# A first stage of attention and MLP whose per-engine order is planned inside the kernel, with a changed two-step activation

## The chip, the cores and the metric

The kernel runs on one core of a Trainium2 chip. Its time is the device time of one execution in microseconds; three runs are shown for the kernel before. TensorE (PE), VectorE (DVE), ScalarE (ACT) and GpSimd (POOL) each work through a queue of their own in a fixed order, and transfers are issued from SyncE (SP).

## The reference

Everything is float32. Attention over 2 batches, 8 heads, 768 positions and 64 channels sees, for each position, the keys less than 16 positions away and the 24 block summaries (blocks of 32 positions; the key's summary is a maximum, the value's a mean). Two MLPs follow on the 1536 tokens of width 512, each with 2048 hidden units.

```python
scores_l = scale * (q @ k.T), where |i - j| < 16, else -1e9
scores_s = scale * (q @ k_sum.T) + log(32)          # k_sum: max over a block
a = exp(scores_all - max); a = a / (sum(a) + 1e-9)
x = a @ concat(v, v_sum)                            # v_sum: mean over a block
h = x @ w_in;  g = maximum(h, 0) + alpha * minimum(h, 0);  x = g @ w_out
h = x @ w2_in; g = h * sigmoid(h);                         out = g @ w2_out
```

## The kernel before

Work on the MLPs is done to nearly full float32 precision with three matmuls in place of one: every operand is split into a rounded high part and a low part, and function three issues low x high, high x low, high x high. Each weight part (128 x 512) is loaded raw, put together by three bitwise VectorE steps into w (lines 142, 146, 149), cast to its high part on ScalarE (line 155), and its low part is a subtraction, on GpSimd in the first stage (line 156).

The first stage takes queries in units of 256 positions (block blk, of six) and one pair of heads (p, of four): 24 units. In a unit, scores does 8 small matmuls, which the compiler issues as 16 (line 523): for each 128 queries, head and half of 64 queries, the 24 block summaries and a window of 96 keys side by side, 120 columns. For that the summaries lie ahead of every window in the key tile, and two instructions prepare it (line 465 the maximum, line 471 copies it to the other windows). Then come the scaled and masked scores t (line 531), the maximum nm (540), four exponentials with their sums (548), a small add and a reciprocal (557, 559), the normalization on GpSimd (560), four transposes (566), their copy (568), the values' matmuls (579), and the high and low parts of x (587, 588). Value summaries take two halving adds on GpSimd (482), a sum on VectorE (485), a transpose (491) and four spreading copies on ScalarE (495).

The first chunk (512 of 2048 hidden units) of the first MLP is done in the same stage, block by block: in_k adds the matmuls of one pair's 128 channels, activate does two rectified copies on ScalarE (324, 325), a multiply-add on VectorE (328), a cast (336) and a subtraction (337); out_pair does the second layer. Block 0's first layer runs pair by pair into four PSUM banks while its units are made. Of the eight banks, six serve all of this in rotation and two the scores.

Order is a list of operations sorted by a key in units of one attention unit (the constants AT_..., CONV, BATCH at the top), which the framework's scheduler then places. Weight loads and the second batch's values share two staging buffers; the first three weight parts and the first batch's values go to a region that is free then. After the stage a loop works through the other chunks and the second MLP with tiles of 512 tokens, converting one weight part every few items on VectorE.

Of the kernel before, what the change touches and what calls it, by code (L numbers as in the profile page):

```python
# [10 lines left out]
F32 = mybir.dt.float32  # L11
# [14 lines left out]
AT_KEYS, AT_SUMS, AT_MEANS, AT_SPREAD = -1.1, 1.3, 2.2, 3.2  # L26
AT_EXPS, AT_NORM, AT_TURN, AT_VALUES = 0.1, 0.3, 1.8, 3.2
AT_IN = 5.3
AT_LATER, ITEM_STEP = 3.5, 0.8
CONV, CONV_STEP = -1.4, 0.6  # L30
CONV2, CONV2_STEP = 14.0, 1.5
BATCH, BATCH_STEP = 5.8, 2.0
NQ = 6
STAGE = 2


@with_exitstack
def tile_blocks_attention_mlps(
# [19 lines left out]
    KEYS = P + 2 * PAD  # L58
# [61 lines left out]
    def conv_next(eng):  # L120
# [33 lines left out]
        def rest():  # L154
            nc.scalar.copy(out=hi, in_=w)  # L155
            eng.tensor_tensor(out=lo, in0=w, in1=hi, op=ALU.subtract)
# [5 lines left out]
        return rest  # L162
# [115 lines left out]
    def three(ps, a, b, first, last):  # L278

        (ah, all_), (bh, bl) = a, b  # L280
        nc.tensor.matmul(ps, all_, bh, start=first, stop=False)  # L281
        nc.tensor.matmul(ps, ah, bl, start=False, stop=False)  # L282
        nc.tensor.matmul(ps, ah, bh, start=False, stop=last)  # L283
# [3 lines left out]
    def in_k(u, i, k, ps):  # L287
        l, ch, t0, n, _ = u
        c = slice(i * P, (i + 1) * P)
        hi, lo = pieces[l, ch, 0, k]  # L290
        three(
            ps, (hi[:, c], lo[:, c]), (xh[:, k, t0:t0 + n], xl[:, k, t0:t0 + n]),
            k == 0, k == KT - 1,
        )
# [9 lines left out]
    def activate(u, i, ni, banks):  # L304

# [14 lines left out]
        if l == 0:  # L320
            m = gp.tile([P, 512], F32, tag="m", name="m", bufs=1 if early else 2)
            w = ni * n // len(banks)
# [3 lines left out]
            for j in range(ni):  # L326
                at = slice(j * n, (j + 1) * n)
                nc.vector.scalar_tensor_tensor(  # L328
                    out=g[:, at], in0=m[:, at], scalar=nal[:, f + j:f + j + 1], in1=g[:, at],
                    op0=ALU.mult, op1=ALU.add,  # L330
                )
        else:
            nc.scalar.activation(out=g, in_=banks[0], func=AF.Silu)

        def rest():
            nc.scalar.copy(out=gh, in_=g)  # L336
            (nc.gpsimd if early else nc.vector).tensor_tensor(out=gl, in0=g, in1=gh, op=ALU.subtract)  # L337

        pending.append(rest)
# [80 lines left out]
    def convert(eng):  # L420
        r = conv_next(eng)
        if r is not None:
            pending.append(r)
# [3 lines left out]
    with ExitStack() as scope0:  # L427
# [7 lines left out]
        mask = cst[:, P:]  # L435

        kt_t, vt_t, vs_t, q_t = {}, {}, {}, {}

        def load_k(b, p):

            t = kv.tile([P, NTWO + 1, NB + KEYS], F32, tag="kT", name="kT")
            nc.sync.dma_start(out=t[:, :NTWO, NB:], in_=kT[b, p])
            kt_t[b, p] = t

        def load_v(b, p):
# [5 lines left out]
            vt_t[b, p] = t  # L451
            t = kv.tile([NC, NSUB, P], F32, tag="vs", name="vs")
            vs_t[b, p] = t
            nc.sync.dma_start(out=t[NB:, 0::2], in_=vw[b, p, 0])
            nc.sync.dma_start(out=t[:WIN, 1::2], in_=vw[b, p, 1])
# [7 lines left out]
        def prep_k(b, p):  # L463
            t = kt_t[b, p]
            nc.vector.tensor_reduce(  # L465
                out=t[:, 0, :NB].rearrange("p (n m) -> p n m", n=NTWO),
                in_=t[:, :NTWO, NB + PAD:NB + PAD + P].rearrange("p n (m i) -> p n m i", i=BLOCK),
# [7 lines left out]
        vr_t = {}  # L475

        def prep_v1(b, p):

            t = kv.tile([P, NB], F32, tag="vr", name="vr", bufs=2)
            v = vt_t.pop((b, p)).rearrange("p (n i) -> p n i", i=BLOCK)  # L480
            for w in (BLOCK // 2, BLOCK // 4):
                nc.gpsimd.tensor_tensor(
                    out=v[:, :, :w], in0=v[:, :, :w], in1=v[:, :, w:2 * w], op=ALU.add
                )
            nc.vector.tensor_reduce(out=t, in_=v[:, :, :w], axis=AX.X, op=ALU.add)
            vr_t[b, p] = t

        def prep_v2(b, p):
            s_ = vs_t[b, p]
# [3 lines left out]
            def spread(s0, s1):  # L493
                for at in (s_[:NB, 2 * s0:2 * s1:2], s_[WIN:, 2 * s0 + 1:2 * s1:2]):
                    nc.scalar.activation(
                        out=at,
                        in_=pt[:NB, 0:P].unsqueeze(1).to_broadcast([NB, s1 - s0, P]),
                        func=AF.Copy,
                        scale=1.0 / BLOCK,
                    )  # L500

            spread(0, QB // P)
            return lambda: spread(QB // P, NTWO)

        e_t, pt_t, sums, t_t = {}, {}, {}, {}

        def where(n):
            blk, p = order[n]
            b, j = divmod(blk, BPB)
            return blk, p, b, j  # L510

        def scores(n):
            blk, p, b, j = where(n)
            q_, k_ = q_t.pop((blk, p)), kt_t[b, p].rearrange("p n c -> p (n c)")

            ps = ps_s.tile([P, 2, 512], F32, tag="s", name="sc")
            for i in range(2):
                for h in range(2):
                    hp = slice(h * D, (h + 1) * D)
# [354 lines left out]
```

## Time and profile before

| | us |
|---|---|
| median of 3 runs | 608.24 (608.11 to 608.34) |
| span of the profiled execution | 604.6 |
| the median less the span | 3.6 |
| TensorE busy | 576.8 (95%) |
| VectorE busy | 424.0 (70%) |
| ScalarE busy | 277.5 (46%) |
| GpSimd busy | 72.3 (12%) |

The profile has one execution. Its own time outside the profiler is not recorded, so its span stands for it, and the 3.6 us between span and median are start and end of the program outside the span. A matmul's end is modelled and matmuls overlap, so a busy TensorE says that it had work, not at which rate; for a rate one takes the distance from one start to the next. Times count from the start of the span.

### The profile page before, as it was taken

What the parts mean: (1) busy time and instruction counts of PE and PEld (TensorE: products, weight loads), DVE (VectorE), ACT (ScalarE), POOL (GpSimd) and SP (SyncE); (2) the same over time, 40 slices, a digit from 0 to 9 for tenths busy, and PEclk for the clock granted to TensorE, in tenths of its full rate; (3) what the DMA queues carried; (4) which work ended last, traced back from release to release, by engine and by line L of the source; (5) the groups of instructions that cost most, each with busy time, mean ns of one, the idle gap of its engine ahead of it and who ended that gap; (6) DMA issues with size and microseconds to landing.
All of it is one profiled execution on the core that took longest, in us unless ns stands there. A gap on an engine that the chain in (4) does not pass through costs nothing.

```text
span 604.6 us, 8927 instructions
## 1 busy us (share of the span) xinstructions
PE 576.8 (95%) x3428; PEld 483.5 (80%) x3428; DVE 424.0 (70%) x747; ACT 277.5 (46%) x636; POOL 72.3 (12%) x69
## 2 busy tenths in 40 slices
PE   2777999999999999999999999999999999999997
PEld 1556788999888888888888888888888888888886
DVE  3899979548995484349696879885972499965312
ACT  2768977654543341424544645543621245333200
POOL 2657654232100000000000000000000000000000
PEclk9988999999999999999999999999999999999999
DMA  9958754002351040003022002333130032200112
GB/s 263 341 193 260 231 147 140 2 2 70 140 154 56 0 140 0 1 1 112 28 69 70 1 1 79 131 117 93 32 108 0 1 111 96 73 1 0 54 69 88
DMA packets 31771, 52.54 MB, mean 87 GB/s; under 512 B 2288, under 2 KB 20976, under 8 KB 31728
## 3 DMA queue, kind: packets, MB, share of 16 engines
q1 hardware_dynamic: 31728, 51.97, 27.2%
q8 instruction: 27, 0.44, 0.3%
q14 instruction: 16, 0.13, 0.1%
HBM read 48.82 MB, written 3.15 MB: 86 GB/s over the span
## 4 chain that ended last, share of the span: by engine, by line
PE 82%; DVE 9%; DMA 3%; ACT 2%; SPq 1%; issue 1%; POOL 0%; DVEq 0%; POOLq 0%
PE ps L281 27%; PE ps L282 27%; PE ps L283 27%; DVE w L146 2%; DMA y<-in_w 1%; DVE w L149 1%; DMA vs<-in_vw 1%; DVE w L142 1%; DVE t L531 1%; DVE sm L557 1%; DVE nm L540 1%; PE o L579 1%; DVE kT L465 1%; ACT e L548 1%; DMA raw<-in_w 1%
## 5 line engine op out<-in xcount | busy, mean ns | idle before, releaser
L281 PE MATMUL ps<-xh,wl 128*128 128x512 f32 (+1 forms) x352 | 127.5, 367 | 1.2 <-ACT xh L587 1.2
L282 PE MATMUL ps<-xl,wh 128*128 128x512 f32 (+1 forms) x352 | 127.9, 364 | 0.0
L283 PE MATMUL ps<-xh,wh 128*128 128x512 f32 (+1 forms) x352 | 127.4, 363 | 0.0
L282 PE MATMUL ps<-gl,wh 128*128 128x512 f32 (+1 forms) x240 | 83.3, 348 | 0.0
L283 PE MATMUL ps<-gh,wh 128*128 128x512 f32 (+1 forms) x240 | 82.9, 346 | 0.0
L281 PE MATMUL ps<-gh,wl 128*128 128x512 f32 (+1 forms) x240 | 82.5, 350 | 0.0
L336 ACT CAST gh<-g 128x512 fp32r<-128x512 f32 x96 | 59.3, 622 | 46.2 <-PE ps L283 24.2
L281 PEld LDWEIGHTS ps<-xh,wl 128*128 128x128 f32 x352 | 66.5, 191 | 12.4 <-POOL e L560 1.4
L282 PEld LDWEIGHTS ps<-xl,wh 128*128 128x128 f32 x352 | 67.3, 191 | 10.2 <-issue 0.2
L283 PE MATMUL ps<-wh,gh 128*128 128x512 f32 (+1 forms) x196 | 75.4, 385 | 0.0
L283 PEld LDWEIGHTS ps<-xh,wh 128*128 128x128 f32 x352 | 67.3, 191 | 10.1
L282 PE MATMUL ps<-wl,gh 128*128 128x512 f32 (+1 forms) x196 | 75.4, 385 | 0.0
L281 PE MATMUL ps<-wh,gl 128*128 128x512 f32 (+1 forms) x196 | 75.2, 385 | 0.1
L337 DVE TENSOR_TENSOR gl<-g,gh 128x512 fp32r<-128x512 f32 x84 | 57.5, 687 | 20.7 <-ACT gh L336 20.3
L394 DVE TENSOR_TENSOR y<-ps,y 128x512 f32<-128x512 f32 x48 | 32.8, 689 | 45.4 <-PE ps L283 45.2
L324 ACT ACTIVATE g<-ps 128x512 f32<-128x512 f32 (+1 forms) x50 | 29.0, 579 | 70.8 <-PE ps L283 69.9
L155 ACT CAST wh<-w 128x512 fp32r<-128x512 f32 x64 | 39.3, 622 | 48.0 <-DVE w L149 43.5
L328 DVE SCALAR_TENSOR_TENSOR g<-m,nal,g 128x512 f32<-128x512 f32 (+1 forms) x60 | 41.4, 705 | 25.0 <-ACT m L325 24.9
L281 PEld LDWEIGHTS ps<-gh,wl 128*128 128x128 f32 x240 | 45.2, 189 | 6.6 <-issue 0.5
L282 PEld LDWEIGHTS ps<-gl,wh 128*128 128x128 f32 x240 | 45.4, 189 | 6.1 <-POOL gl L337 0.2
L283 PEld LDWEIGHTS ps<-gh,wh 128*128 128x128 f32 x240 | 45.3, 189 | 5.6
L146 DVE SCALAR_TENSOR_TENSOR w<-raw,w 128x512 uint32<-128x512 uint32 x61 | 44.6, 741 | 0.3
(82 smaller groups left out, 867.1 us busy)
## 6 DMA issues: line engine op xcount, KB each, us to landing
raw<-in_w SPq DMA_DIRECT2D x61, 512.0 KB, 3.8
vs<-in_vw SPq DMA_DIRECT2D x16, 288.0 KB, 5.6
kT<-in_kT SPq DMA_DIRECT2D x8, 480.0 KB, 5.2
q<-in_qT SPq DMA_DIRECT2D x24, 128.0 KB, 4.1
out<-y SPq DMA_DIRECT2D x11, 256.0 KB, 2.0
y<-in_vT SPq DMA_DIRECT2D x4, 384.0 KB, 6.5
y<-in_w SPq DMA_DIRECT2D x3, 512.0 KB, 7.7
raw<-in_vT SPq DMA_DIRECT2D x4, 384.0 KB, 4.5
```

The source lines that it names most:

```text
L142: nc.vector.tensor_scalar(out=w, in0=high, scalar1=3, scalar2=0x3FFFFFFF, op0=ALU.logical_shift_left, op1=ALU.bitwise_and,)
L146: nc.vector.scalar_tensor_tensor(out=w, in0=high, scalar=0xC0000000, in1=w, op0=ALU.bitwise_and, op1=ALU.bitwise_or)
L149: nc.vector.scalar_tensor_tensor(out=w, in0=low, scalar=29, in1=w, op0=ALU.logical_shift_right, op1=ALU.bitwise_or)
L155: nc.scalar.copy(out=hi, in_=w)
L281: nc.tensor.matmul(ps, all_, bh, start=first, stop=False)
L282: nc.tensor.matmul(ps, ah, bl, start=False, stop=False)
L283: nc.tensor.matmul(ps, ah, bh, start=False, stop=last)
L324: nc.scalar.activation(out=g[:, j * w:(j + 1) * w], in_=ps, func=AF.Relu)
L328: nc.vector.scalar_tensor_tensor(out=g[:, at], in0=m[:, at], scalar=nal[:, f + j:f + j + 1], in1=g[:, at], op0=ALU.mult, op1=ALU.add,)
L336: nc.scalar.copy(out=gh, in_=g)
L337: (nc.gpsimd if early else nc.vector).tensor_tensor(out=gl, in0=g, in1=gh, op=ALU.subtract)
L394: nc.vector.tensor_tensor(out=at, in0=src, in1=at, op=ALU.add)
```

## The change

The first stage is no longer a sorted list for the framework's scheduler. Every step (a load, a preparation, one operation of a unit, one conversion step, a pair of hidden rows, an output pair) is declared with its engine, an assumed cost, the steps that it follows, a key, and what it takes and gives back of the buffers (PSUM banks, tiles, staging buffers). The function plan then plays the engines forward: again and again it places the step that can start first, and among those that could start within 0.03 us the one with the lowest key. Conversions on VectorE and work on GpSimd are kept apart by a common lock in the plan, and transfers by an assumed rate. The steps are issued in the order of their planned starts, and that is the order in which each engine runs them.

Beside it:

- The activation is h + (1 - alpha) max(-h, 0): one rectified copy m on ScalarE, and the multiply-add on VectorE reads h from PSUM. This holds for all chunks of the first MLP.
- Summaries stand once in the key tile; scores issues, for each 128 queries and head, one matmul of 24 columns over all 128 queries and two of 96 columns over 64 queries. The keys come unstacked (128 x 800), and a pair's value windows in one load instead of two.
- Value summaries are one sum over 32 positions on VectorE; the halvings are gone. Spreading takes two instructions instead of four.
- The 1e-9 stands in a second column beside each sum; a reduction over two columns replaces the add.
- Blocks 0 and 1 both run their first layer pair by pair, two hidden rows in one PSUM bank, two banks each.
- Two items of the next chunk's first layer run inside the stage instead of one just behind it.

```diff
-AT_KEYS, AT_SUMS, AT_MEANS, AT_SPREAD = -1.1, 1.3, 2.2, 3.2
...
+AT_KEYS, AT_SUMS, AT_MEANS, AT_SPREAD = -1.1, 1.82, 2.2, 1.7
+AT_EXPS, AT_NORM, AT_TURN, AT_VALUES = 0.26, 0.73, 1.37, 3.2
+CONV, CONV_STEP = -1.08, 0.76
+CONV2, CONV2_STEP = 17.32, 2.66
+W_FIRST, W_STEP, W_AHEAD = -98.82, 1.32, -2.52
+SLACK, RATE = 0.03, 0.34
+AHEAD, AT_NEXT = 2, 3.49
...
-                nc.scalar.activation(out=g[:, j * w:(j + 1) * w], in_=ps, func=AF.Relu)
                 nc.scalar.activation(out=m[:, j * w:(j + 1) * w], in_=ps, func=AF.Relu, scale=-1.0)
...
                 nc.vector.scalar_tensor_tensor(
-                    out=g[:, at], in0=m[:, at], scalar=nal[:, f + j:f + j + 1], in1=g[:, at],
-                    op0=ALU.mult, op1=ALU.add,
+                    out=g[:, at], in0=m[:, at], scalar=nal[:, f + j:f + j + 1],
+                    in1=ps[:, j * n % w:j * n % w + n], op0=ALU.mult, op1=ALU.add,
                 )
...
-            nc.vector.tensor_copy(
-                out=t[:, 1:, :NB], in_=t[:, 0:1, :NB].to_broadcast([P, NTWO, NB])
-            )
...
+                for h in range(2):
+                    hp = slice(h * D, (h + 1) * D)
+                    nc.tensor.matmul(
+                        ps[:, h, i * NC:i * NC + NB],
+                        q_[hp, i * P:(i + 1) * P],
+                        k_[hp, KEYS:KEYS + NB],
...
-                            ps[s * SUB:(s + 1) * SUB, h, i * NC:(i + 1) * NC],
+                            ps[s * SUB:(s + 1) * SUB, h, i * NC + NB:(i + 1) * NC],
                             q_[hp, i * P + s * SUB:i * P + (s + 1) * SUB],
-                            k_[hp, w0:w0 + NC],
+                            k_[hp, w0:w0 + WIN],
...
+        room = {"sc": 1, "mm": 6, "t": 3, "e": 3, "pT": 2, "q": NQ, "k": 4, "v": 4, "vr": 2,
+                "raw": STAGE, "w": 2, "g": 1, "gh": 3}
...
+        for n in range(3 * CF + STAGE):
+            t = W_FIRST + n * W_STEP if n < 2 * CF else max(W_FIRST + n * W_STEP, CONV2 + (n - 2 * CF) * CONV2_STEP - W_AHEAD)
+            load(("W", n), t, load_next, size=0.52, after=[("W", n - 1)] * (n > 0),
+                 take=["raw"] * (n >= y_w.shape[1]))
...
+            step(("sc", *g), "PE", 0.8, [("K", b, p), ("q", *g)], k + AT_SC, scores, *g,
+                 take=["sc"], give=["q"] + ["k"] * last)
+            step(("mk", *g), "DVE", 0.58, [("sc", *g), "cst"], k + AT_MASK, masked, *g,
+                 take=["t"], give=["sc"])
...
+            step(("e", *g), "POOL", 0.95, [("rs", *g)], k + AT_NORM, normalize, *g, lock=True)
+            step(("pt", *g), "PE", 0.45, [("e", *g)], k + AT_TURN, turn, *g,
+                 take=["mm"], give=["e"])
...
+            step(("cv", n), "DVE", 1.65, [("W", n)] + [("cv", n - 1)] * (n > 0), t, bits, n,
+                 take=["w"], give=["raw"] * (n >= y_w.shape[1]), lock=True)
...
+        def plan():
+            end, free, hold = {}, dict.fromkeys(("SP", "PE", "ACT", "DVE", "POOL"), 0.7), {}
...
+                        at = max([free[e], *(end[x] for x in after)])
+                        for r in take:
+                            at = max(at, sorted(hold[r])[take.count(r) - 1])
+                        if lock:
+                            at = max(at, locked)
...
+                        t0 = min(at for at, _ in found)
+                        at, s = min(((at, s) for at, s in found if at <= t0 + SLACK), key=lambda x: x[1][:2])
...
+        with tc.manual_schedule():
+            for _, _, f, a in plan():
+                f(*a)
```

## Rows read from the trace of the kernel before

**Rows 1.** Busy time by stretch: span, its length, then per engine (instructions), clock, DMA share, GB/s.
```profile
0.00:40.00 40.00, 22.81 (x220) 17.40 (x221) 28.80 (x56) 20.82 (x70) 19.25 (x23) 0.96 0.93 278
40.00:64.00 24.00, 17.13 (x250) 13.47 (x250) 23.96 (x48) 21.18 (x81) 15.05 (x14) 0.93 0.72 220
64.00:104.00 40.00, 39.50 (x450) 34.76 (x451) 35.06 (x70) 31.68 (x96) 22.27 (x20) 1.00 0.61 176
```

**Rows 2.** The chain of waits: start, length (us), what.
```profile
15.52 7.75 DMA y<-in_w
23.29 1.19 DVE w L142
...
75.95 3.81 DMA raw<-in_w
...
102.46 0.63 PE sc L523 x14
```

**Rows 3.** Timeline of TensorE where it is full: start, length, what.
```profile
117.63 0.64 PE L523 MATMUL sc<-kT,q 64*64 64x120 f32 x16
118.20 0.69 PE L579 MATMUL o<-pT,vs 120*64 120x64 f32 x16
118.82 0.65 PE L566 MATMUL pt<-cst,e 128*120 128x128 f32 x4
119.40 0.69 PE L579 MATMUL o<-pT,vs 120*64 120x64 f32 x16
120.01 0.38 PE L281 MATMUL ps<-xh,wl 128*128 128x256 f32 x1
120.24 0.28 PE L282 MATMUL ps<-xl,wh 128*128 128x256 f32 x1
120.35 0.28 PE L283 MATMUL ps<-xh,wh 128*128 128x256 f32 x1
```

**Rows 4.** TensorE's groups, 0 to 64 us: busy, mean ns; idle before, releasers.
```profile
L523 PE MATMUL sc<-kT,q 64*64 64x120 f32 x224 | 13.1, 346 | 13.5 <-DVE kT L465 5.7 <-DVE t L531 3.4 <-DVE vr L485 3.3
L566 PE MATMUL pt<-cst,e 128*120 128x128 f32 x44 | 9.3, 350 | 7.2 <-POOL e L560 5.2 <-POOL wl L156 1.3 <-DVE xl L588 0.7
L579 PE MATMUL o<-pT,vs 120*64 120x64 f32 x144 | 8.6, 280 | 2.2 <-DVE xl L588 1.9 <-ACT m L325 0.3
...
L281 PE MATMUL ps<-xh,wl 128*128 128x256 f32 x18 | 5.2, 377 | 1.2 <-ACT xh L587 1.2
```

**Rows 5.** Transfers, GB/s in each microsecond from 0 to 40 us.
```profile
GB/s 0 0 147 352 342 315 327 281 267 298 321 405 306 253 325 377 337 343 386 289 297 309 407 414 343 373 348 257 295 336 343 368 373 176 116 12 0 86 291 303
```

**Rows 6.** Groups of other engines by shape, 0 to 130 us.
```profile
L531 DVE SCALAR_TENSOR_TENSOR t<-sc,cst 128x480 f32<-128x480 f32 x24 | 15.5, 646 | 6.6 <-PE sc L523 6.5
...
L328 DVE SCALAR_TENSOR_TENSOR g<-m,nal,g 128x256 f32<-128x256 f32 x18 | 11.8, 693 | 1.8 <-ACT m L325 1.8
...
L557 DVE TENSOR_SCALAR sm<-sm 128x4 f32<-128x4 f32 x24 | 9.0, 374 | 4.7 <-ACT e L548 4.7
...
L588 DVE TENSOR_TENSOR xl<-o,xh 128x256 fp32r<-128x256 f32 x21 | 8.6, 412 | 0.4 <-ACT xh L587 0.3
...
L465 DVE TENSOR_REDUCE kT<-kT 128x24 f32<-128x768 f32 x8 | 7.5, 943 | 6.4 <-DMA kT<-in_kT 6.4
...
L324 ACT ACTIVATE g<-ps 128x512 f32<-128x512 f32 x7 | 4.1, 590 | 3.4 <-PE ps L283 2.9 <-POOL gl L337 0.5
...
L471 DVE COPY kT<-kT 128x144 f32<-128x144 f32 x8 | 2.9, 358 | 0.0
...
L485 DVE TENSOR_REDUCE vr<-y 128x24 f32<-128x192 f32 x4 | 1.4, 344 | 2.4 <-POOL y L482 2.4
```

**Rows 7.** VectorE's conversion steps by shape: 0 to 64 us, then 150 to 200 us (two rows).
```profile
L146 DVE SCALAR_TENSOR_TENSOR w<-raw,w 128x512 uint32<-128x512 uint32 x6 | 6.6, 1100 | 0.0
...
L146 DVE SCALAR_TENSOR_TENSOR w<-raw,w 128x512 uint32<-128x512 uint32 x10 | 6.8, 684 | 0.0
L142 DVE TENSOR_SCALAR w<-raw 128x512 uint32<-128x512 uint32 x8 | 4.1, 515 | 2.0 <-DMA raw<-in_w 1.9
```

More of the change, by code (lines that the diff above doesn't have):

```diff
@@ L290, in in_k @@
         hi, lo = pieces[l, ch, 0, k]
-        three(
+        return three(
             ps, (hi[:, c], lo[:, c]), (xh[:, k, t0:t0 + n], xl[:, k, t0:t0 + n]),
-            k == 0, k == KT - 1,
+            k == 0 if first is None else first, k == KT - 1, first is not None,
         )
@@ L304, in activate, with activation @@
     def activate(u, i, ni, banks):
+        one, two, *rest = activation(u, i, ni, banks)
+        one()
+        two()
+        pending.extend(rest)
+    def activation(u, i, ni, banks):
         l, ch, t0, n, _ = u
@@ L730, in seq_item, with step, load @@
-        def seq_item():
-            need(CF if seq[0][1] is in_item else 2 * CF)
-            item()
-        def more_loads():
-            for _ in range(CF):
-                ask(None)
+        where = {g: k for k, g in enumerate(order)}
+        steps = []
+        def step(name, engine, cost, after, key, f, *a, take=(), give=(), lock=False, size=0):
+            steps.append((key, len(steps), name, engine, cost, after, f, a, take, give, lock, size))
+        def load(name, key, f, *a, size, after=(), take=()):
+            step(name, "SP", 0.6, after, key, f, *a, take=take, size=size)
@@ new lines, in tile_blocks_attention_mlps, with first_in, whole_in @@
+        acc, acts = {}, {}
+        def first_in(blk, p, i):
+            if blk not in acc:
+                acc[blk] = [ps_mm.tile([P, 512], F32, tag="mm", name="ps") for _ in range(CF // 2)]
+            for i in range(0, CF, 2) if i is None else [i]:
+                ps = acc[blk][i // 2]
+                in_k(units[blk], i, p, ps[:, :QB], p == 0)
+                in_k(units[blk], i + 1, p, ps[:, QB:], False)
+        def whole_in(blk, i):
+            ps = ps_mm.tile([P, 512], F32, tag="mm", name="ps")
+            acc.setdefault(blk, {})[i // 2] = ps
+            for j in range(2):
+                for k in range(KT):
+                    in_k(units[blk], i + j, k, ps[:, j * QB:(j + 1) * QB])
@@ new lines, in tile_blocks_attention_mlps, with next_in @@
+        ahead = []
+        def next_in(f):
+            ps = ps_mm.tile([P, 512], F32, tag="mm", name="ps")
+            for k in range(KT):
+                in_k(units[NBLK], f, k, ps)
+            ahead.append(ps)
+        for f in range(AHEAD):
+            step(("nx", f), "PE", 2.72, [("lo", 3 * CF - 1)] + [("x", blk, p) for blk in range(TB // QB)
+                 for p in range(NPAIR)] + [("nx", f - 1)] * (f > 0), NG + AT_NEXT + f, next_in, f, take=["mm"])
+        def plan():
+            end, free, hold = {}, dict.fromkeys(("SP", "PE", "ACT", "DVE", "POOL"), 0.7), {}
+            for r, n in room.items():
+                hold[r] = [0.0] * n
+            left = {e: sorted(s for s in steps if s[3] == e) for e in free}
+            locked, wire, out = 0.0, 0.0, []
+            while any(left.values()):
+                best = None
+                for e, todo in left.items():
+                    found = []
+                    for s in todo[:60]:
+                        key, _, name, _, cost, after, f, a, take, give, lock, size = s
+                        if any(x not in end for x in after):
+                            continue
+                        if any(len(hold[r]) < take.count(r) for r in take):
+                            continue
+                        at = max([free[e], *(end[x] for x in after)])
[3 more added lines that the diff above has]
+                            at = max(at, locked)
+                        if size:
+                            at = max(at, wire - 6.5)
+                        found.append((at, s))
+                    if found:
+                        t0 = min(at for at, _ in found)
+                        at, s = min(((at, s) for at, s in found if at <= t0 + SLACK), key=lambda x: x[1][:2])
+                        if best is None or at < best[0]:
+                            best = at, s
+                at, s = best
+                key, _, name, e, cost, after, f, a, take, give, lock, size = s
+                left[e].remove(s)
+                out.append((at, s[1], f, a))
+                free[e] = at + cost
+                if lock:
+                    locked = at + cost
+                for r in take:
+                    hold[r].remove(min(hold[r]))
+                end[name] = at + cost + (0.25 if e == "PE" else 0.12)
+                if size:
+                    wire = max(wire, at + 1.4) + size / RATE
+                    end[name] = wire + 0.9
+                for r in give:
+                    hold[r].append(end[name])
+            return sorted(out, key=lambda x: x[:2])
@@ L780, in tile_blocks_attention_mlps @@
     ps_o.append(ctx.enter_context(tc.tile_pool(name="ps_o", bufs=2, space=bass.MemoryType.PSUM)))
+    for f in range(AHEAD):
+        activate(units[NBLK], f, 1, [ahead[f]])
+        convert(nc.vector)
+        rests()
     due = 0.0
```

397 lines of the change are left out of this document (196 added, 201 removed).

## The prediction

> **What bounds the kernel now.** Start with the busy time by stretch [rows 1]. From 64 us on TensorE is busy in 39.5 of 40 us, and it stays so to the end of the program; before 40 us it is busy in 22.8 of 40 us, and VectorE, at 23.96 of 24 us between 40 and 64, is full. The chain of waits [rows 2] says the same in order of time: a weight's transfer ends at 23.3 us, VectorE's conversion starts there, VectorE's steps make up most of the chain until 84 us, and from 102.5 us it is TensorE alone. So the program is TensorE-bound with a late start, and the question is how late.
>
> A busy TensorE early on is not one at its rate, so I count work instead. At full rate [rows 3] a score group takes 0.57 us (117.63 to 118.20), a values group 0.61, a transpose group 0.58 and elsewhere about 0.4 (I take 0.5), a 256-column matmul 0.12 (120.35 from 120.24). Up to 64 us TensorE issued [rows 4] 224/16 = 14 score groups, 11 transpose groups, 9 values groups and 52 matmuls of 256 columns (18 of line 281's, 17 each of lines 282 and 283): 8.0 + 5.5 + 5.5 + 6.2 = 25.2 us, with four small transposes about 26. **The lag at 64 us is 64 - 26 = 38 us.** After that TensorE waits 0.5 us in the next 40, so nearly every microsecond taken from the lag comes off the end. The whole first stage is 24 x (0.57 + 0.5 + 0.61) + 576 x 0.12 + 1.6 = 111 us of TensorE.
>
> Of the 38 us only some must be. At 30 us the sum of the transfer rates [rows 5] is 9.05 MB. The first two blocks need four pairs of k, v, v-windows and two q tiles (1.64 MB each) plus the constants and four first-layer weight parts (2.4 MB): 9.0 MB. They were all there near 30 us, yet 34 us later, at 64 us, only 52 of the 96 matmuls that they feed had run.
>
> **The change part by part.** VectorE first, since it holds the chain.
> - Copies of the key maxima to the other windows (line 471) go: 8 x 0.358 = 2.9 us [rows 6].
> - The two halvings on GpSimd go and VectorE's sum reads 768 columns instead of 192. The nearest row is the maximum over 768, 0.943; the sum over 192 takes 0.344 [rows 6]: 8 x 0.6 = 4.8 us more. GpSimd loses 16 instructions, which no longer sit between a transfer and the sum.
> - The small add before the reciprocal takes 374 ns [rows 6]. It becomes a reduction of eight numbers, bounded by today's 0.374 and by nearly nothing; taken 0.17, half of a sum over 192 columns, which is mostly fixed cost: 24 x 0.2 = 4.9 us less.
> - The activation's multiply-add, 24 in this stage, reads h from PSUM. Today 693 ns with both inputs in SBUF; the nearest with one input in PSUM and 256 columns is the low half of x, 412 [rows 6]. Bounds 0.41 and 0.69, taken 0.43: 6.3 us less.
> - The planner holds conversions and GpSimd's work apart. The second conversion step took 1100 ns before 64 us and 684 when GpSimd is quiet [rows 7]; over three steps about 0.6 us, 12 times: 0 to 7 us less, taken 5.
> VectorE's stage thus loses 14 us (it is busy 88 up to 104 us [rows 1]), but before 64 us only some 5 of 53 (eight copies, eleven small adds, nine conversions, less six longer sums). Work removed is not the main effect; order is.
>
> ScalarE loses one Relu per pair (0.59 [rows 6], 7 us in 12 pairs) and half of its spreading instructions; in later chunks 36 more Relus go. I cost these at nothing: ScalarE is busy 31.7 of 40 us while TensorE is full [rows 1]. Without that cover it is the 7 us. In return the PSUM bank stays held through VectorE's step, about 0.4 us longer, hidden by the other banks; uncovered 12 x 0.4 = 5 us. The accumulators of block 0 (four banks) become two banks for each of blocks 0 and 1: four of six either way.
>
> On the queue of transfers each pair's v-window loads become one and keys shrink from 480 to 400 KB: 0.3 MB in the first eight units, about 1 us; the first weight is now asked for ahead of pair 1's values, and the loads for the second batch follow the buffers as they come free. Nothing else is put ahead of a load that the first unit needs.
>
> The scores are the cost on TensorE. A unit has 16 issued matmuls of 120 columns; it will have 16 of 96 and 8 of 24 over all 128 output columns. Bounds: 0.57 (work alone: 16 x 120 against 16 x 96 + 8 x 24 x 2 columns) and 0.57 x 24/16 = 0.86 by count. Taken 0.75, nearer the count since 24 columns is short of every row seen: +0.18 x 24 = **+4.3 us** (0 to 7).
>
> Now the order. (a) First phase, to the end of blocks 0 and 1's first-layer matmuls. Data are there at 30 us. VectorE's part [rows 6, 7] is 8 x 2.0 for units (mask 0.65, the maximum over the same columns as much, two small steps of 0.17, low half 0.41), 4 x 1.9 for key maxima and sums, and 5 x 1.9 for conversions (0.515 + 2 x 0.684): 33 us. It can start when the first key tile has landed, at 4.7 us, so 38 us at best. That leaves it no idle time. In the first 40 us it now idles 11.2 [rows 1], 4.7 of them for the first key; of the other 6.5 I allow 4, so 42. TensorE has then done 8 x 1.86 + 0.8 + 96 x 0.12 = 27 us: lag 15. (b) Until the second-layer weights are converted, which I put at about 48 (three more parts through two buffers, a chain wait of 3.81 at most for one [rows 2], half overlapped), only units 8 to 11 and block 2 can run, 13 us of work in bits as VectorE feeds it: 5 us more. (c) From there on, per unit, TensorE has 1.86 + 2.9 (24 matmuls of 0.12) = 4.7 us, and VectorE 2.0 plus a share of keys and sums 0.5, conversions 0.8, multiply-adds 0.4 and output copies 0.35 = 4.1: TensorE full, with little to spare. **Lag 20 against 38: 18 us less.** Bounds: 11 (38 us, nothing in b) and 33 (52 us, 8 in b).
>
> Sum: -18 + 4.3 = -13.7. The profiled execution has a span of 604.6 us; the median of the runs is 608.24, so 3.6 us lie outside the span and stay. Span 591, time **594.5 us**. The likeliest case alone: 587 to 601.
>
> What follows the stage is left as it is: two items of the next chunk run ahead instead of one, and TensorE is full there already.
>
> A rule against the change, beside the rows. After a group of small tiles the first full matmul starts the next one 0.23 us later instead of 0.12 (120.01 to 120.24 [rows 3]): about 0.11 us to change over. The new score group goes from 64x128 tiles to 64x64 tiles twice, three change-overs inside a unit that had none. The Trainium skill, TensorEngine Tiling (Array Packing), Key Properties, says that a change of tiling mode, not just of tile, drains TensorE. By that rule the sum would be 0.33 x 24 = 8 us for the drains on top, 602.5; by the count alone 594.5.
>
> **The rivals.**
> 1. The drains (above): 3 x 0.11 x 24 = 8 us on top of the 4.3: 602.5. For: the 0.11 us is seen. Against: values and transposes, of different tiles too, follow each other from 118.20 to 120.01 at 0.6 each [rows 3], as quick as where they stand alone. Chance 0.10.
> 2. VectorE stays the bound of the first 64 us. For: it loses only 5 of 53 us there, and its sums grow. Then the lag falls by those 5 and by some 4 from order, less 4.3: about 604. Against: block 0 and 1's matmuls need only eight units, and nothing forces the other work ahead of them. Chance 0.15.
> 3. Slower, by one mechanism: VectorE stands behind a conversion whose weight has not landed. From the fourth weight on, nine conversions and four v loads share two buffers. The chain shows one such wait of 3.81 us at 75.95 [rows 2], and behind it on VectorE's queue stand the masked scores and maxima of the next units, for which TensorE, ScalarE and GpSimd wait. The order is fixed by planned landing times, so a plan that is early blocks again and again. At 3.81 each the gain is gone with the fourth; with six, 23 us against 13.7: 617. Against: the transfers are busy 0.61 of the time from 64 to 104 us [rows 1], so there is room on the wire, and only one such wait is on the chain of a kernel with the same two buffers. Chance 0.13.
> 4. No change: the order gets TensorE full earlier by just what the scores cost (lag 34): 608. Chance 0.05.
>
> **How the numbers follow.** Forecast 0.57; with rivals 1 and 2 faster in 0.82; within 0.2% (1.2 us, about what a measurement of this kernel can tell from no change) 0.05; slower 0.13. The range of 8 in 10 runs from 584 (lag 12 with scores at 2 us) to 607, which takes in rivals 1 and 2 and leaves out rival 3 and the ends.
>
> **What would show it.** Right: 256-column matmuls of the first layer start near 15 us, when one unit's chain and one weight can be through; counted as above, the lag at 64 us is near 20; the small reduction stands near 0.17, the multiply-add near 0.43; a score group takes 0.75. Wrong: VectorE idle ahead of the first conversion step with a transfer as the releaser several times (rival 3); VectorE full to 64 us with under 90 matmuls of 256 columns done (2); a score group near 1.0 (1). What would make the prediction wrong altogether is a wait on PSUM banks, of which two serve transposes, values and means while the accumulators hold four, as they do now.

## The result, and the profile after

The changed kernel takes 613.57 us (median of 4 runs, 612.1 to 614.3) against 608.17 for the kernel before beside it: a ratio of 1.0085, 95% interval 1.0061 to 1.011. It is slower where 594.5 was forecast, and the time lies outside the range of 584 to 607. The profiled execution has a span of 611.9 us against 604.6, 7.3 more, where the medians differ by 5.4. In every execution that has both numbers on record (all but the profiled one of the kernel before) the time is 1.7 to 1.9 us longer than the span. So the profiled execution before took some 606.4 us, less than its median: half of the 3.6 us that the prediction adds to the span is that, and not start and end of the program.

Busy time by stretch after, columns as in [rows 1]:

```profile
0.00:40.00 40.00, 26.46 (x278) 20.66 (x279) 20.81 (x45) 19.06 (x64) 7.80 (x12) 1.00 0.88 247
40.00:64.00 24.00, 24.00 (x303) 20.52 (x299) 19.00 (x42) 16.33 (x59) 7.38 (x7) 0.86 0.50 163
64.00:104.00 40.00, 38.54 (x462) 33.85 (x463) 34.55 (x74) 32.34 (x104) 22.07 (x19) 0.91 0.65 190
```

Against [rows 1] the two engines have changed places: from 40 to 64 us VectorE is busy 19.0 us where it was full, and TensorE is full where it was busy 17.1. Read as shares this is just what was wanted. The next two views say what TensorE is full with. The chain of waits after (start, length, what) runs early through TensorE's scores, where [rows 2] has VectorE's steps:

```profile
21.33 0.56 PE sc L533 x4
21.89 0.53 PE sc L544 x8
22.41 0.55 PE sc L533 x4
22.97 0.53 PE sc L544 x8
```

And the timeline of TensorE where it runs at the full granted clock, as in [rows 3]:

```profile
99.58 0.41 PE L533 MATMUL sc<-kT,q 64*128 64x24 f32 x4
99.91 0.40 PE L544 MATMUL sc<-kT,q 64*64 64x96 f32 x8
100.24 0.41 PE L533 MATMUL sc<-kT,q 64*128 64x24 f32 x4
100.57 0.40 PE L544 MATMUL sc<-kT,q 64*64 64x96 f32 x8
100.90 0.39 PE L287 MATMUL ps<-gh,wl 128*128 128x256 f32 x1
101.12 0.28 PE L288 MATMUL ps<-gl,wh 128*128 128x256 f32 x1
```

From the first start to that of the full matmul behind it, a unit's scores take 100.90 - 99.58 = **1.32 us, where they took 0.57** and 0.75 was forecast. TensorE's groups from 0 to 64 us, as in [rows 4]:

```profile
L533 PE MATMUL sc<-kT,q 64*128 64x24 f32 x102 | 13.3, 337 | 9.5 <-DVE kT L488 5.7 <-issue 1.9 <-DMA q<-in_qT 1.8
L544 PE MATMUL sc<-kT,q 64*64 64x96 f32 x200 | 12.5, 332 | 0.0
L287 PE MATMUL ps<-xh,wl 128*128 128x256 f32 x28 | 9.8, 350 | 0.0
...
L596 PE MATMUL pt<-cst,e 128*120 128x128 f32 x40 | 8.0, 335 | 0.0
L612 PE MATMUL o<-pT,vs 120*64 120x64 f32 x144 | 7.5, 260 | 1.1 <-ACT pT L601 1.1
```

Counted as in the prediction, with 1.32 for a score group and 0.2 for each of four small transposes: 12.6 units x 1.32 + 10 x 0.5 + 9 x 0.61 + 84 x 0.12 + 0.8 = 38.0 us of work, a lag of 26 at 64 us (38 before, 20 forecast). The order did bring TensorE forward, if by less than forecast; 84 full matmuls stand there instead of 52. The same count up to 104 us gives a lag of 62.1 to 104 = 41.9 before and 104 - 72.9 = 31.1 after. So the order is worth 10.8 us where the stage gets full, the scores cost 24 x (1.32 - 0.57) = 18.0, and 18.0 - 10.8 = **7.2 us**, against the 7.3 by which the span has grown. The prices are rounded, so the last tenth is luck, but the same count up to 104 us also comes near the spans of the first three runs below: 1.9, 5.1 and 4.6 us less than before, measured 2.1, 5.2 and 4.7.

VectorE's groups by shape up to 130 us, which answer to [rows 6, 7]:

```profile
L150 DVE SCALAR_TENSOR_TENSOR w<-raw,w 128x512 uint32<-128x512 uint32 x11 | 9.6, 870 | 0.3
...
L347 DVE SCALAR_TENSOR_TENSOR g<-m,nal,ps 128x256 f32<-128x256 f32 x16 | 6.9, 475 | 3.4 <-ACT m L341 3.4
...
L146 DVE TENSOR_SCALAR w<-raw 128x512 uint32<-128x512 uint32 x11 | 5.5, 504 | 2.5 <-DMA raw<-in_w 2.5
...
L507 DVE TENSOR_REDUCE vr<-y 128x24 f32<-128x768 f32 x4 | 3.8, 946 | 1.2 <-DMA y<-in_vT 1.2
...
L583 DVE TENSOR_REDUCE rs<-eps 128x4 f32<-128x8 f32 x23 | 3.5, 152 | 2.5 <-ACT e L574 2.3
```

The small reduction takes 152 ns (0.17 forecast), the multiply-add 475 (0.43), the sum over 768 columns 946 (0.943), the second conversion step 870, only in part down to its quiet 684: it is 692 in all five conversions before 64 us and 909 in the nine from there to 130.

SyncE's transfers after, in order of issue:

```profile
17.19 0.33 SPq L120 DMA_DIRECT2D y<-in_w  x1
...
31.84 0.42 SPq L120 DMA_DIRECT2D y<-in_w  x1
35.04 1.87 SPq L472 DMA_DIRECT2D raw<-in_vT  x2
48.48 0.33 SPq L464 DMA_DIRECT2D kT<-in_kT  x1
49.39 0.37 SPq L120 DMA_DIRECT2D raw<-in_w  x1
```

The third weight is asked for at 31.84 us and the fourth, the last that the first layer needs, at 49.39: between them two loads of the second batch's values take both staging buffers. The kernel before had asked for its second weight at 15.52 us, for its third at 17.74 and for the fourth here:

```profile
22.71 3.43 SPq L116 DMA_DIRECT2D raw<-in_w  x1
```

### The profile page after: what moved, and what is told of

Same layout as the page of the kernel before. It is cut to its first block, busy times and chain, and to the rows that moved or that the text cites. A ratio compares the mean times of both kernels' runs of the same rounds, so it can differ in the third digit from the quotient of the medians.

```text
span 611.9 us, 9208 instructions
## 1 busy us (share of the span) xinstructions
PE 593.4 (97%) x3620; PEld 499.5 (82%) x3620; DVE 415.3 (68%) x743; ACT 252.6 (41%) x568; POOL 56.1 (9%) x53
## 4 chain that ended last, share of the span: by engine, by line
PE 93%; issue 3%; DMA 1%; DVE 1%; SPq 0%; POOL 0%; POOLq 0%; ACT 0%
PE ps L287 28%; PE ps L288 27%; PE ps L289 27%; PE sc L533 3%; PE sc L544 3%; PE pt L596 2%; PE o L612 2%; DMA q<-in_qT 1%; POOL gl L356 0%; DVE w L150 0%; POOLq L976 0%; DVE t L556 0%; ACT pT L601 0%; DVE y L426 0%; DVE g L347 0%
## 5 line engine op out<-in xcount | busy, mean ns | idle before, releaser
L287 PE MATMUL ps<-xh,wl 128*128 128x512 f32 (+1 forms) x352 | 130.5, 371 | 0.0
L289 PE MATMUL ps<-xh,wh 128*128 128x512 f32 (+1 forms) x352 | 128.7, 366 | 0.0
L287 PEld LDWEIGHTS ps<-xh,wl 128*128 128x128 f32 x352 | 68.4, 194 | 10.8 <-issue 0.2
L288 PEld LDWEIGHTS ps<-xl,wh 128*128 128x128 f32 x352 | 68.6, 195 | 9.8
L341 ACT ACTIVATE m<-ps 128x512 f32<-128x512 f32 x48 | 28.7, 597 | 86.3 <-PE ps L289 86.0
L347 DVE SCALAR_TENSOR_TENSOR g<-m,nal,ps 128x512 f32<-128x512 f32 (+1 forms) x60 | 37.2, 637 | 27.1 <-ACT m L341 27.1
L574 ACT ACTIVATE e<-t,nm 128x120 f32<-128x120 f32 x96 | 36.7, 384 | 18.3 <-DVE nm L567 16.2
```

What stands on the lines that cost most here:

```text
L287: i = nc.tensor.matmul(ps, all_, bh, start=first, stop=False, skip_group_check=again)
L288: nc.tensor.matmul(ps, ah, bl, start=False, stop=False, skip_group_check=again)
L289: nc.tensor.matmul(ps, ah, bh, start=False, stop=last, skip_group_check=again)
L347: nc.vector.scalar_tensor_tensor(out=g[:, at], in0=m[:, at], scalar=nal[:, f + j:f + j + 1], in1=ps[:, j * n % w:j * n % w + n], op0=ALU.m ...
L574: nc.scalar.activation(out=e[:, u, :], in_=t[:, u, :], func=AF.Exp, bias=nm[:, u:u + 1], accum_out=sm[:, u, 0:1],)
```

## The experiments: the scores

The theory: a unit's scores now go back and forth between two tile shapes, and TensorE pays at each change. The rival: it pays by the number of instructions, 24 instead of 16. The first three runs keep the changed kernel and alter the scores alone.

**All 24-column matmuls first**, then all of 96 columns: one change in a unit instead of three, the same 24 instructions, the same plan.

```diff
             for i in range(2):
                 for h in range(2):
                     hp = slice(h * D, (h + 1) * D)
                     nc.tensor.matmul(
                         ps[:, h, i * NC:i * NC + NB],
...
+            for i in range(2):
                 for h in range(2):
```

> The changed kernel with one edit: in a unit's scores all four 24-column matmuls come first, then the eight of 96 columns; the same 24 issued instructions, but one change between tile shapes inside the group instead of three. Drain theory (each change of shape costs about 0.2 us, which is what 1.32 us less the 0.57 of the old group leaves for it): the group falls to about 0.95 us, 24 x 0.37 = 9 us less, time near 604.5. Count theory (0.055 us for each of 24 instructions): group 1.32, time 613.5 within 1. Order theory (the loss is waiting and not the scores): the group may fall but the time stays within 2 of 613.5.

606.92 us, ratio 0.9974 (0.9952 to 0.9996). TensorE's timeline of this kernel:

```profile
113.57 0.63 PE L533 MATMUL sc<-kT,q 64*128 64x24 f32 x8
114.12 0.56 PE L545 MATMUL sc<-kT,q 64*64 64x96 f32 x16
114.61 0.69 PE L613 MATMUL o<-pT,vs 120*64 120x64 f32 x16
```

A unit takes 114.61 - 113.57 = 1.04 us, 0.28 less for two changes less: 0.14 each. Over 24 units that is 6.7 us, and the ratio fell by 0.0111, 6.7 us.

**Small tiles for the short matmuls**: 64 of the 128 queries at a time, so that all have the 64x64 shape. That makes 32 instructions and no change inside a unit; the plan stays.

```diff
-                        ps[:, h, i * NC:i * NC + NB],
-                        q_[hp, i * P:(i + 1) * P],
...
+                    for s in range(2):
...
+                            ps[s * SUB:(s + 1) * SUB, h, i * NC:i * NC + NB],
+                            q_[hp, i * P + s * SUB:i * P + (s + 1) * SUB],
```

> The changed kernel with the 24-column matmuls cut to 64x64 tiles as the windows' are: 32 issued instructions a unit instead of 24, no change of shape inside the group. Drain theory: group about 0.6 to 0.75 us, 24 x 0.6 = 14 us less, time near 599. Count theory: 32 x 0.055 = 1.76 us, 24 x 0.44 = 10.5 us more, time near 624. Order theory: within 2 of 613.5.

**600.68 us, ratio 0.9853 (0.9827 to 0.9879).** Its timeline of TensorE:

```profile
100.58 0.31 PE L534 MATMUL sc<-kT,q 64*64 64x24 f32 x8
100.72 0.38 PE L545 MATMUL sc<-kT,q 64*64 64x96 f32 x8
100.91 0.26 PE L534 MATMUL sc<-kT,q 64*64 64x24 f32 x8
101.00 0.37 PE L545 MATMUL sc<-kT,q 64*64 64x96 f32 x8
101.30 0.39 PE L287 MATMUL ps<-gh,wl 128*128 128x256 f32 x1
```

101.30 - 100.58 = 0.72 us: with a third more instructions than the changed kernel a unit takes 0.60 us less, 14.4 us over 24; the ratio fell by 0.0232, 14.1 us. The count theory falls. Of the 0.75 us that a unit had grown, 0.28 went with two changes of shape, 0.32 with the third and with the 64x128 tile itself (these two runs don't part them), and 0.15 stays. (The median itself fell by 12.9 us and the span by 12.5; the ratios are taken to the kernel before beside each run.)

**Summaries stacked ahead of each window again**, in the changed kernel's plan: 16 instructions of 120 columns.

```diff
+            nc.vector.tensor_copy(
+                out=t[:, 1:, :NB], in_=t[:, 0:1, :NB].to_broadcast([P, NSUB - 1, NB]))
...
-                            k_[hp, w0:w0 + WIN],
+                            k_[hp, 2 * (2 * j + i) + s],
```

> The changed kernel with the scores of the kernel before: the summaries are copied ahead of each of 12 stacked windows of 96 keys, and a unit has 16 issued matmuls of 120 columns in 64x64 tiles. Eight VectorE copies of some 0.35 us come back and a pair's keys are 590 KB instead of 400. Drain and count theories alike: group 0.57 us, 24 x 0.75 = 18 us less, 2 to 4 us back for copies and loads, time near 597. Order theory: within 3 of 613.5.

602.0 us, ratio 0.9881 (0.9854 to 0.9907). A unit takes 0.57 us again (101.25 to 101.82), 18 us less in all; only 12.4 are measured. The count puts the rest into a larger lag, 37.3 at 104 us where the changed kernel has 31.1. That this comes from the copies on VectorE, and not from the larger loads of keys, is not shown.

**The new scores and layout alone in the kernel before.**

> The kernel before with the new scores alone (24 and 96 columns, keys and value windows laid out for them, no copies of summaries), order and activation as before. If the scores cost 0.75 us a unit more: about 10 units lie where TensorE is full, 7.5 us more, less what VectorE saves with the copies, time 613 to 616; if they cost nothing that shows (order theory): within 2 of 608.2.

631.12 us, ratio 1.0358 (1.0332 to 1.0384): 22 us slower, well above the 613 to 616 expected. The price of 1.32 a unit gives 18 of them (in its timeline too the four rows of a unit start 0.33 us apart: 100.91, 101.25, 101.57, 101.91), and the count up to 140 us has a lag of 49.4 against 43.5 before. Where one of its units is broken up, groups of other sizes stand between changes of shape:

```profile
124.44 0.40 PE L515 MATMUL sc<-kT,q 64*128 64x24 f32 x2
124.77 0.39 PE L526 MATMUL sc<-kT,q 64*64 64x96 f32 x6
```

The next matmul, of the full shape, starts at 125.09. So two matmuls of 24 columns take 0.33 us and six of 96 take 0.32, and in the changed kernel four of 24 and eight of 96 take 0.33 each. With small tiles eight of 96 take 0.19 with the same shape behind them (100.72 to 100.91) and 0.30 with another (101.00 to 101.30). In these rows a short group that ends in a change of shape takes 0.30 to 0.33 us, whichever of these it holds, and four such groups make the 1.32. Only the eight of 24 columns in the first run take more, 0.55 (113.57 to 114.12).

## The experiments: the order

With small tiles a unit costs 0.72 us, what the prediction had taken (0.75), so that kernel should have come near 594. It took 600.7 and, **measured again** beside the last run below, 599.5.

> The run with small tiles for the short matmuls once more, as the measure for the run with halved v loads on the same chip: a ratio near 0.985 and 599 to 602 us by the theory that the changes between tile shapes cost the scores their time; a ratio near 1 if the first measurement was a chance of its chip.

Ratio 0.9849 (0.9818 to 0.988): it holds. The windows of the first of these two runs, with two stretches of 4 us:

```profile
0.00:40.00 40.00, 25.33 (x482) 20.82 (x482) 27.61 (x61) 24.87 (x87) 11.01 (x15) 1.00 0.94 268
40.00:64.00 24.00, 19.57 (x382) 16.67 (x379) 22.75 (x52) 21.00 (x72) 12.20 (x12) 0.96 0.88 264
64.00:104.00 40.00, 37.34 (x457) 34.65 (x456) 32.87 (x65) 26.41 (x80) 19.51 (x17) 0.89 0.44 129
...
68.00:72.00 4.00, 1.65 (x52) 1.35 (x50) 3.90 (x9) 2.09 (x4) 1.39 (x2) 1.00 0.39 113
72.00:76.00 4.00, 3.69 (x61) 2.84 (x53) 3.90 (x7) 4.00 (x17) 2.06 (x2) 0.56 0.71 214
```

TensorE's work counted as above is again 38.0 us at 64 us (16 units x 0.72 + 13 x 0.5 + 12 x 0.61 + 96 x 0.12 + 1.2), lag 26. At 104 us it is 70.8, lag 33.2: 8.7 less than before, 3.6 of dearer scores, so 5.1 us; the span fell by 5.2 (599.4). VectorE is nearly full until 64 us and transfers are too. At 64 us this stands on VectorE's timeline:

```profile
63.95 0.65 DVE L557 SCALAR_TENSOR_TENSOR t<-sc,cst 128x480 f32<-128x480 f32 x1
68.00 0.43 DVE L146 TENSOR_SCALAR w<-raw 128x512 uint32<-128x512 uint32 x1 [3.40 <-DMA raw<-in_w]
```

VectorE waits 3.4 us for a weight that the chain has in flight for 8.43 us from 59.55. TensorE runs dry from 68 to 72 (1.65 busy of 4) and then works at a granted clock of 0.56, near the lower of its two levels (1.2 of 2.4 GHz). The profiled execution of the second run, with a span of 598.7, has this otherwise: VectorE waits 1.81 us for the same weight and 2.53 for an earlier one, TensorE is busy 3.36 of 4 us from 68 to 72, and the clock from 72 on is 1.00. So neither the dry stretch nor the slow one behind it is needed for the time of this kernel. Theories for what holds the stage: late weights, the two staging buffers, VectorE's amount, the rate of the loads. Each was tried, from the small-tile kernel unless said.

**Weights earlier**: a load follows the issue of the one before, not its landing, and the second batch's values take one staging buffer at a time. First with small tiles, then with the changed scores, then with small tiles and the scores' planned cost at 0.6 instead of 0.8.

```diff
-            load(("W", n), t, load_next, size=0.52, after=[("W", n - 1)] * (n > 0),
+            load(("W", n), t, load_next, size=0.52, after=[("Wi", n - 1)] * (n > 0),
...
-                load(("vt", b, p), t + 1.5, load_vt, b, p, size=0.39, take=["raw"])
+                load(("vt", b, p), t + 1.5, load_vt, b, p, size=0.39, take=["raw", "rv"])
```

> The second experiment's kernel (summaries in 64x64 tiles) with two edits of the planner's rules: a weight part's load has to follow only the issue of the one before it, not its landing, and the second batch's v loads may hold one of the two staging buffers, not both. Load theory (both buffers go to v loads at about 33 us, so the fourth weight part is asked for at 38.7 us and the eighth at 59.6, and the second layer waits for them; the chain there is transfers and conversions from 34 to 68 us): the fourth follows the third at once, the eighth is converted near 50 us, 7 to 10 us less, time 591 to 594. Rival (VectorE is full from 32 to 64 us anyway, 0.9 of the time, and sets the pace): within 2 of 600.7.

> The changed kernel, its scores as they are, with the same two edits of the load order alone. Load theory in full: 5 to 8 us less, time 606 to 609. If the scores alone set the pace (TensorE is on the chain from 12 us to the end): within 2 of 613.5. So this tells how much of the changed kernel's own loss is the loads'.

> The fifth kernel with the planner's price of a score group at 0.6 us, as measured with small tiles, instead of 0.8, so that the plan's order is made for the group that runs. Theory that a wrong price misorders the queues: 1 to 3 us under the fifth. Rival (0.2 us in a group changes nothing that matters): within 1 of the fifth.

605.36 (0.9953, 0.9925 to 0.9982), 616.12 (1.0121, 1.0081 to 1.0161) and 606.29 (0.996, 0.9937 to 0.9984): with small tiles slower than without the edit, with the changed scores not faster (the intervals overlap).

**Staging buffers freed**: the second batch's values in two tiles of their own; then with the issue order too; then both with the changed kernel's scores.

```diff
-                t = stage.tile([P, 512, 2], F32, name="raw")...
+                t = kv.tile([P, S], F32, tag="vx", name="vx", bufs=2)
```

> The small-tiles kernel with the second batch's values loaded to two tiles of their own instead of the two staging buffers that the weights use. Buffer theory (13 loads go through two buffers between 30 and 85 us, the eighth weight part is asked for at 59.6 us and TensorE is short of work from 60 to 80 us): weights flow, TensorE is busier from 60 to 80 us, 3 to 8 us less, 593 to 598. Rival (the loads are not what is short there): within 1.5 of 600.7.

> The kernel of the run before with a weight's load following the issue and not the landing of the one before it. Buffer theory: as good as the run before or 1 to 3 us better, 591 to 597. Rival (VectorE, given more conversions early, makes the units late, as in the fifth run): 603 to 607.

> The changed kernel, scores as they are, with both edits of the loads (own place, issue order). Buffer theory: 2 to 5 us less than 613.5, 608 to 612. Rival (the scores keep TensorE on the chain whatever the loads do): within 2 of 613.5.

606.39 (0.9934, 0.9911 to 0.9957), 611.46 (1.0032, 1.0004 to 1.006) and 626.69 (1.0278, 1.0231 to 1.0325): slower again. In the last, the window from 40 to 104 us has a granted clock of 0.76 with TensorE busy 59.90 of 64 us.

**Less work on VectorE**: sums over 8 of 32 positions, which leaves out three quarters of every value mean; then the halvings back on GpSimd.

```diff
-  step(("vr", b, p), "DVE", 0.87, [("vt", b, p)], k + AT_SUMS, sum_v, b, p, BLOCK,
+  step(("vr", b, p), "DVE", 0.87, [("vt", b, p)], k + AT_SUMS, sum_v, b, p, BLOCK // 4,
```

> The second experiment's kernel (small tiles) with the value sums taken over the first 8 of each 32 positions alone: it leaves out three quarters of the value means, in the same order of steps, and nothing is put in their place. VectorE has 8 x 0.6 = 4.8 us less to do, six of the eight sums before 70 us. VectorE theory (it is busy 30.1 of 32 us from 32 to 64 us and sets the pace there): 3 to 5 us less, time 596 to 598. Rival (loads or the order set it): within 1 of 600.7.

> The small-tiles kernel with the two halvings of the values back on GpSimd, as before the change, as planned steps of 1.7 us under the common lock, and VectorE's sum over 192 columns. VectorE theory: 8 x 0.6 us of VectorE go, but a halving stands between a landing and the sum, and GpSimd blocks conversions: 1 to 4 us less, 597 to 600. Rival: no gain or up to 3 us more, the sum being the longer way.

600.11 (0.9829, 0.9788 to 0.9869) and 601.79 (0.9858, 0.9826 to 0.9889). The short sum takes 0.34 us instead of 0.95, 4.8 us less over eight with the plan unchanged, and the time doesn't answer beyond the intervals.

**The v loads in halves**, plan unchanged.

```diff
-            nc.sync.dma_start(out=t[NB:], in_=vw[b, p])
+            for s in (slice(0, NSUB // 2), slice(NSUB // 2, NSUB)):
+                nc.sync.dma_start(out=t[NB:, s], in_=vw[b, p, :, s])
```

> The kernel of the run with small tiles for the short matmuls (600.7 us), with each v load of two heads' windows cut into two loads of half its bytes, and the plan unchanged. If the stage's loads are what holds it until about 70 us, because the long packets of the merged load land slowly (9.1 us for 576 KB, where the kernel before moved its smaller loads at 278 GB/s in the first 40 us), the halves land earlier and the run takes 596 to 599 us. The rival, by which the order of the steps and not the rate of the loads holds the stage: within 1 us of the same kernel with whole loads, run beside it.

599.08 us, ratio 0.9841 (0.9814 to 0.9868), within 1 us of its measure: the rival. The loads land a little earlier but the rate in the first 40 us is 263 GB/s against 268. From its profile's list of DMA issues (KB each, us to landing; 576 KB in 8.6 with whole loads), and two of its windows:

```profile
vs<-in_vw SPq DMA_DIRECT2D x16, 288.0 KB, 7.2
```

```profile
64.00:72.00 8.00, 6.44 (x73) 5.67 (x73) 5.13 (x14) 5.12 (x16) 2.74 (x3) 0.79 0.76 202
72.00:80.00 8.00, 6.95 (x123) 6.07 (x113) 7.83 (x17) 8.00 (x29) 4.69 (x6) 1.00 0.64 203
```

The half-rate stretch from 72 us on is not there (the clock is 0.79 from 64 to 72), but nor is it in the second run of the kernel with whole loads, so the halves can't be credited with that. The time is the same.

**The old activation.** First with its own costs and bank release in the plan, then with the halvings on GpSimd too; then the same old instructions in exactly the small-tile kernel's order; last the new activation alone in the kernel before.

```diff
+                nc.scalar.activation(out=g[:, j * w:(j + 1) * w], in_=ps, func=AF.Relu)
...
-                    in1=ps[:, j * n % w:j * n % w + n], op0=ALU.mult, op1=ALU.add,
+                    in1=g[:, at], op0=ALU.mult, op1=ALU.add,
```

> The small-tiles kernel with the activation of the kernel before (two Relus on ScalarE, the multiply-add on SBUF alone; the PSUM bank given back after ScalarE). If reading h from PSUM holds banks behind VectorE's full queue (the eighth experiment was 0.4% slower with it): 1 to 3 us less, 598 to 600. If it only saves: ScalarE gets 7 us more and VectorE up to 24 x 0.2 us: 601 to 604.

> Both edits of the two runs before on the small-tiles kernel. VectorE theory and the bank theory together: 595 to 599; if each costs: 602 to 606.

> The small-tiles kernel with the old activation's instructions and the plan left as it is (same prices, same order of steps on every engine). If the 12 us of the eleventh run are the activation itself: about 612. If they are the other order that the plan made of its prices: 600 to 604.

> The kernel before with the new activation alone: one Relu less for each pair, the multiply-add reads h from PSUM. Costed at nothing on ScalarE and 0.27 us less on VectorE for each of 24 multiply-adds, which are on the chain only in places: time 606 to 608.5. If the PSUM banks held longer cost what I put as uncovered: up to 5 us more, 613.

613.19 (1.0046, 1.0014 to 1.0079), 620.15 (1.0156, 1.012 to 1.0192), 603.0 (0.9902, 0.9866 to 0.9937) and 611.79 (1.0042, 1.0024 to 1.006). In one order the new activation is worth 0.0049 of 608, some 3 us, with intervals that just overlap. The first and the third run hold the same instructions and differ in their order alone: 0.0144, 8.8 us. In the kernel before, where the framework's scheduler places the steps, the new activation gains nothing and costs 2.6 us; whether by the order or by the banks held longer is not parted.

## Why the prediction was wrong

- **The step that failed** is the term of the scores, "Taken 0.75 ... +4.3 us (0 to 7)". It measured 0.75 us on top of 0.57, so +18.0, outside both bounds. The bounds were made from columns and from count, and the measure refutes count: 32 instructions take 0.72 us and 24 take 1.32. What the prediction had beside them as a rule, and gave 0.10, was the mechanism of at least 0.28 of the 0.75 us: tiles of another shape don't follow each other freely. The Trainium skill, TensorEngine Tiling (Array Packing), Key Properties, says that a change of tiling mode drains TensorE; the trace agrees, with 0.14 us for each of the two changes that could be taken out by themselves. Rival 1 was mis-sized as well: 8 us on top, against 13.7.
- The evidence against it was misread. Values and transposes do follow each other at 0.6, but a group of 16 that pays one change can't show what a group of 4 or 8 pays for each (sixteen of 96 columns ahead of another shape take 0.49 us in the first run, eight take 0.33 in the changed kernel).
- **The order**, "Lag 20 against 38: 18 us less", had the mechanism right and the size wrong: 12 us by 64 us, and 10.8 left at 104. The phase (a) that was to end at 42 us had its 96th matmul of 256 columns only near 56 us with small tiles and near 67 us after; at 42 us 24 of them had run, as many as before. The first such matmul stood at 28.4 us, not near 15. "Data are there at 30 us" was read from the kernel before (with the new keys of 400 KB in the sum; its own 480 make it some 1 us later) and did not hold for the new plan, which asked for the third weight at 31.84 us and for the fourth at 49.39, since two loads of values had taken both staging buffers at 35.04. The sentence "Nothing else is put ahead" looked only at what the first unit needs. With small tiles the sum of VectorE's steps left out that units beyond the eight run in between, 16 in the first 64 us.
- **TensorE early.** Phase (a) took VectorE as its limit and TensorE's work at full-rate prices. After, the chain of waits from 12.08 to 34.01 us is TensorE's groups but for 3.1 us, and they run at the slow rate told in the last section until 33.2 us: TensorE is busy 20.65 us up to there with what the count prices at 11.8. The kernel before has such a stretch too, up to 33 us, but there VectorE holds the chain; with small tiles it ends at 21.7 us.
- "From there on TensorE full, with little to spare" failed by 5 us after 64 us (lag 26 to 31), where 4 are lost before too (38 to 41.9), with TensorE full at a granted clock of 1.00, so that much the count's prices leave out. After, the clock is 0.91 there and TensorE idles 1.5 us.
- **Rival 2** (VectorE stays the bound) is half seen: with small tiles VectorE is busy 22.75 of 24 us to 64 us, yet less work on it gave nothing. **Rival 3** has a clear case with small tiles, 3.4 us in one execution and 1.81 in the other; in the changed kernel the first conversion step waited 2.5 us in all for its data up to 130 us. It isn't what made the kernel slow.
- VectorE's prices held, the conversions aside: fourteen of them up to 130 us take 29.8 us where they took 32.5, so of the taken 5 us about half is seen, and all of it before 64 us. The old activation in the same order costs 3 us: ScalarE's Relu, costed at nothing, and the longer multiply-add together.
- The sum's last term, 3.6 us outside the span, is 1.8 in the executions that show it; the forecast would have been 592.8.
- The remaining 6 us between the small-tile kernel and 594 are **not settled**. Less VectorE work, other places for the weights, more staging room and halved loads gained nothing beyond the intervals, and of the nine runs in which these edits let the planner make a new order, seven were slower than the run they stand beside, by 5 to 18 us; two (the weights earlier with the changed scores, the halvings on GpSimd) were the same within their intervals. That shows only that the order found for exactly these costs is better than its neighbours, not which wait is left in it.

The changed kernel with small tiles takes 0.985 of the time of the kernel before, so it beats both the kernel before and the changed one.

## What to carry to other kernels

Before columns or instructions of a small matmul are counted, list the tile shapes in the order in which TensorE meets them: here small groups of alternating shapes cost more than a third more instructions of one shape (1.32 us against 0.72). Time a group from its first start to the start of the full matmul behind it, since the busy column shows TensorE full either way. When a planner sets the order, compare an edit in an unchanged plan: the same instructions in another order took 8.8 us more here, as much as most of the edits were meant to win.

## What the runs showed beside

- A stretch can have a granted clock of 1.00 in its row and all of TensorE's groups at about half their rate. From 0 to 40 us the changed kernel's row says 1.00, but its chain has 2.16 us for a unit's scores (21.33 to 23.49) where 1.32 is the price at 97 to 101 us, and matmuls of 256 columns start 0.22 us apart where full rate has 0.12:

```profile
28.80 0.42 PE L288 MATMUL ps<-xl,wh 128*128 128x256 f32 x1
29.02 0.41 PE L289 MATMUL ps<-xh,wh 128*128 128x256 f32 x1
...
43.80 0.41 PE L288 MATMUL ps<-xl,wh 128*128 128x256 f32 x1
44.02 0.42 PE L289 MATMUL ps<-xh,wh 128*128 128x256 f32 x1
```

The second pair stands where the granted clock is 0.50, the lower level (40 to 46 us), and a unit's scores take 2.16 us there too (40.21 to 42.37). At 33.2 us the rate rises in the middle of a unit, with TensorE busy on both sides. So the row seems to miss a lower clock before 33.2 us: the same rates for every shape speak for it, though no row shows the clock itself. The distance from start to start tells the rate; the row alone doesn't.
- The same instructions in another order cost 8.8 us with small tiles; with the changed scores another order and one moved buffer cost 11.7 (626.69, ratio 1.0278 against 1.0085). Both come with less of the granted clock in the stage (0.83 against 0.96 from 64 to 104 us; 0.76 from 40 to 104, where the changed kernel has 0.86 and 0.91 in its two parts).
